# A gated mix of a Fourier layer and a SwiGLU layer: the work up to the second chunk put in a written order

## The chip, the cores and the metric

The kernel runs on one core of a Trainium2 chip. Its time is the device time of one execution in microseconds (us). The time before is the median of three runs.

A core has a matrix engine (TensorE, PE in the profile, with PEld for the loading of its stationary operand), a vector engine (VectorE, DVE), an engine for functions of one operand (ScalarE, ACT), GpSimd (POOL), which only issues stores here, and SyncE (SP), which issues the loads. Each takes its own instructions in the order in which the program has them, and waits at an instruction until what it needs is there. PE writes to eight banks of PSUM; everything else lies in SBUF.

## The reference, cut to what matters

```python
x = A_x                                             # 2048 x 512
g = sigmoid((x * gate_w).sum(-1, keepdims=True))
a = x @ dft_hid_re.T                                # Fourier layer
b = x @ dft_hid_im.T
A = dft_seq_re @ a - dft_seq_im @ b
h = silu(x @ w1) * (x @ w3)                         # SwiGLU layer, F = 1376
B = h @ w2
out = g * A + (1 - g) * B
```

## The kernel before

All is float32. A matrix that is multiplied is split in two parts that PE can take: a *high* part (a copy on ACT, line 108) and a *low* part (the source less the high part, on DVE, line 111). A product of 128x128 by 128x512 is then three matmuls: high by high, high by low, low by high (`mm3`, line 117).

Products of blocks go by a scheme with seven products instead of eight (Strassen's in Winograd's form). Each operand is cut in four blocks, A11 to A22 of the weights and B11 to B22 of x, and sums of blocks are made: T1 = B12 - B11, T2 = B22 - T1, T3 = B22 - B12, T4 = B21 - T2 of x (lines 203 to 207), and four sums of the weights (`sums_wb`, lines 244 to 251). T2, T3 and T4 are written over the raw B11, B12 and B21.

The first stage computes silu(x w1) * (x w3) for the first half of x. It runs over chunks of 128 columns of w1 and w3 (`ITEMS`, line 180). Chunk n has the products X, Y and Z, each a bank of PSUM: X<sub>n</sub> in bank n mod 4, Y<sub>n</sub> in bank 4 + n mod 2, Z<sub>n</sub> in bank 6 + n mod 2. A block of six matmuls (`prod`, line 270) is A11 B11 (`first1`, into X), A12 B21 (`first2`, into Y), and then in `gate_up(n)` (line 332), in this order: X += sum x T2, Z = sum x T3, `first1(n + 3)`, X += sum x T1, Z += a block x T4, `first2(n + 3)`, X += sum x B22. Between them stand ACT's and DVE's work on chunk n and the preparation of the weights of chunk n + 1 (the sums, WB, with `sums_wb`, `high_wb`, `low_wb`) and of chunk n + 4 (the plain blocks, WA). So in `gate_up(1)` chunk 4's `first1` and `first2` are multiplied and the weights of chunk 5 are split; chunk 5's `first1` is multiplied in `gate_up(2)`.

Chunk 0 does without the scheme. `plain` (line 401) computes its four blocks C00, C10, C01, C11 with eight halves of six matmuls each, as the blocks of x arrive: B11, B21, B12, B22. Its result h, 128x1024, is stored by POOL in two halves (`store_h`, line 317). There are two buffers of h: chunk 0 has one, T1 the other, chunk 1 takes chunk 0's.

Weights come as tiles of four blocks of 128x256 (`load_w`, line 221; four such tiles in turn), x as four tiles of 128x1024 (`load_xo`). All loads are on SyncE's queue, in order.

The lines 392 to 488 hold the work up to `gate_up(1)`: loads, eleven matmuls on zeros, chunk 0, A11 B11 and A12 B21 of chunks 1 to 3, the sums and splits of x, and WB of chunk 1. They are written in an order, but the framework's scheduler is free to interleave these lines and does: in the trace, two matmuls of X of chunk 1 stand inside a half of chunk 0. Only from line 674 on (`manual_schedule`) are the instructions of each engine issued as they are written. The lists `early`, `mid` and `at_end` (line 326) hold extra work that `gate_up(n)` runs at three places.

Of the kernel before, what the change touches and what calls it, by code (L numbers as in the profile page):

```python
# [32 lines left out]
def fnet_swiglu_gate_kernel(  # L33
# [46 lines left out]
    def bank(k, name):  # L80
        return psum.tile([P, 512], F32, tag=f"ps{k}", name=name)
# [31 lines left out]
    def split(hi, lo, src):  # L113
        high(hi, src)
        low(hi, lo, src)

    def mm3(ps, ah, al, bh, bl, first, last, chain=False):
        for n, (u, v) in enumerate(((ah, bh), (ah, bl), (al, bh))):
            nc.tensor.matmul(ps, u, v, start=first and n == 0, stop=last and n == 2,  # L119
                             skip_group_check=chain)  # L120
# [115 lines left out]
    def prep_wa(w, lo=0, hi=3):  # L236

        if lo == 0:
            WA[w] = wap.tile([P, 2, 3, 256], F32R, tag="wa", name=f"wa{w}")
        split(*wa_parts(w, lo, hi))  # L240

    WU = {}

    def sums_wb(w):

        r = WS.pop(w)
        u = WU[w] = wup.tile([P, 4, 256], F32, tag="wu", name=f"wu{w}")
        nc.vector.tensor_add(u[:, 0], r[:, 3], r[:, 2])
        nc.vector.tensor_sub(u[:, 1], u[:, 0], r[:, 0])
        nc.vector.tensor_sub(u[:, 2], r[:, 0], r[:, 3])  # L250
        nc.vector.tensor_sub(u[:, 3], r[:, 1], u[:, 1])
# [13 lines left out]
    def prep_wb(w):  # L265
        sums_wb(w)
        high_wb(w)
        low_wb(w)
# [12 lines left out]
    def first1(n):  # L281
        x = bank(n % 4, f"X{n}")
        prod(x, n, 0, 0, True)
        s1 = s1p.tile([P, 512], F32, tag="s1", name=f"s1_{n}")
        nc.scalar.activation(s1, x, AF.Copy)
        G[n] = (x, s1)

    def first2(n):

        y = bank(4 + n % 2, f"Y{n}")  # L290
        prod(y, n, 1, 1, True)
        s1 = G[n][1]
        nc.vector.tensor_add(s1, s1, y)
        put_score(n, 0, s1)
# [28 lines left out]

    early, mid, at_end = {}, {}, {}

    def run(work, n):
        for f in work.get(n, ()):
# [2 lines left out]
    def gate_up(n):  # L332
        last = NI - 1
        x, s1 = G.pop(n)
        z = bank(6 + n % 2, f"Z{n}")
        if n == last - 1:

            u2, g1 = (s1p.tile([P, 512], F32, tag="s1", name=f"{k}_{n}") for k in ("u2", "g1"))
        else:
            h = hp.tile([P, 1024], F32, tag="h", name=f"h{n}")  # L340
            u2, g1 = h[:, :512], h[:, 512:]
        u4 = u4p.tile([P, 512], F32, tag="u4", name=f"u4_{n}")
        nw = WSET[n + 1] if n < last else 0
# [12 lines left out]
        nc.scalar.activation(u2, x, AF.Copy)  # L356
        run(early, n)
        prod(z, n, 5, 5, True, True)
        nc.scalar.activation(u4, z, AF.Copy)
        if nw is not None:  # L360
            sums_wb(nw)
        if n + LOOK <= last:
            first1(n + LOOK)
        if nw is not None:
            high_wb(nw)
        prod(x, n, 3, 3, False, True)
        nc.vector.tensor_add(u4, u4, x)  # L367
        if nw is not None:
            low_wb(nw)
        run(mid, n)  # L370
        prod(z, n, 2, 6, False, True)
        nc.vector.tensor_add(u2, u2, z)
        nc.vector.tensor_mul(u2, s1, u2)  # L373
        store_h(n, 0, u2)
        if wa is not None:
            WA[wa] = wap.tile([P, 2, 3, 256], F32R, tag="wa", name=f"wa{wa}")
# [24 lines left out]
    def plain(b12, a21):  # L401

        c = {}

        def half(i, j, w, x, start):
            if start:
                c[i, j] = bank((0, 4, 6, 7)[2 * i + j], f"C{i}{j}")
            for r in range(2):
                sl = slice(r * P, (r + 1) * P)
                mm3(c[i, j], w(0, sl), w(1, sl), x(r, 0), x(r, 1), start and r == 0,  # L410
                    not start and r == 1)

        def wa(k):
            return lambda h, sl: WA[0][:, h, k, sl]

        def xb(k):
            return lambda q, h: XO[0][:, h, k, q, :]

        w21 = lambda h, sl: a21[:, h, sl]
        x12 = lambda q, h: b12[:, h, q * 512 : (q + 1) * 512]  # L420
        s1 = s1p.tile([P, 512], F32, tag="s1", name="s1_0")
        g1 = u4p.tile([P, 512], F32, tag="u4", name="g1_0")
        h = hp.tile([P, 1024], F32, tag="h", name="h0")
        yield half(0, 0, wa(0), xb(0), True)
        yield half(1, 0, w21, xb(0), True)
        half(0, 0, wa(1), xb(1), False)
        nc.scalar.activation(s1, c[0, 0], AF.Silu)
        yield half(1, 0, wa(2), xb(1), False)
        nc.vector.tensor_mul(h[:, :512], s1, c[1, 0])
        store_h(0, 0, h[:, :512])  # L430
        half(0, 1, wa(0), x12, True)
        yield half(1, 1, w21, x12, True)
        half(0, 1, wa(1), xb(2), False)
        nc.scalar.activation(g1, c[0, 1], AF.Silu)
        half(1, 1, wa(2), xb(2), False)
        nc.vector.tensor_mul(h[:, 512:], g1, c[1, 1])
        yield store_h(0, 1, h[:, 512:])
# [11 lines left out]
    step = plain(b12, a21)  # L449
    prep_wa(0, 0, 1)  # L450
    for q in range(2):
        split(XO[0][:, 0, 0, q], XO[0][:, 1, 0, q], ST[0, "B11"][:, q * 512 : (q + 1) * 512])
    next(step)
    split(a21[:, 0], a21[:, 1], WS[0][:, 3])
    next(step)
    prep_wa(0, 1, 3)
    split_xo(0, "B21")
    next(step)
    split(b12[:, 0], b12[:, 1], ST[0, "B12"])
    next(step)  # L460
    split_xo(0, "B22")
    next(step)
    free(*zt)
    WS.pop(0)
    load_w(4)
    prep_wa(1)
    first1(1)
    first2(1)
    gate1(1)
    sum_xo(0, "T1", hp.tile([P, 1024], F32, tag="h", name="t1"))  # L470
    sum_xo(0, "T2", ST[0, "B11"])
    prep_wa(2)
    first1(2)
    first2(2)
    gate1(2)
    split_xo(0, "T2")
    prep_wb(1)
    sum_xo(0, "T3", ST[0, "B12"])
    split_xo(0, "T3")
    prep_wa(3)  # L480
    first1(3)
    first2(3)
    gate1(3)
    split_xo(0, "T1")
    prep_wa(4)
    sum_xo(0, "T4", ST[0, "B21"])
    split_xo(0, "T4")
    free(*(ST[0, b] for b in ("B11", "B21", "B12", "B22")))

    def do(work, n, f, *a):  # L490
        work.setdefault(n, []).append(lambda: f(*a))


    for k in ("B11", "B21", "B12", "B22"):
# [176 lines left out]
        sum_c(m + LEAD + 1)  # L671
        split_c(m + LEAD)

    ctx.enter_context(tc.manual_schedule())
    for n in range(1, NI):
        gate_up(n)
        if ITEMS[n] == (NC - 1, 0):
# [317 lines left out]
```

## Time and profile before

| | us |
|---|---|
| median of three runs | 711.27 (711.21 to 711.48) |
| profiled execution, its own time | 710.88 |
| span of the profiled execution | 709.1 |
| PE busy | 703.9 (3089 matmuls) |
| DVE busy | 604.6 |
| ACT busy | 369.6 |
| granted PE clock, mean | 1.0 |

The span is that of the instructions on the core; 1.8 us of the execution's time lie around it. Times in the timeline count from the start of the span. A row of it has the start, the duration, the engine, the line, the operation with its output and inputs, and in brackets the idle time of the engine before it with what ended that. `xo` are the split blocks of x, `wa` and `wb` the split weights, `ws` and `xs_B` the raw ones, `C` the banks of chunk 0. Matmuls overlap: one lasts 0.39, and the next starts before it ends. Since line 111 (or 108, or 119) is a helper's, rows of one line are told apart by their tiles.

### The profile page before, as it was taken

To read this page: it belongs to the slowest core of one execution; us is meant where nothing else is said; L and a number is where in the kernel's file an instruction comes from. 1 tells how busy PE (TensorE), PEld (TensorE's weight loads), DVE (VectorE), ACT (ScalarE), POOL (GpSimd) and SP (SyncE) were. 2 spreads that over 40 slices of the span, in tenths; PEclk is the share of its full clock that TensorE was granted. 3 is DMA by queue.
4 is the path that set the end of the run, shared out by engine and by line. 5 is a ranking of instruction groups with operands and counts; after the bars stand their busy time and mean duration, and the time that the engine had idled before them with its cause. 6 is when DMAs were issued, how large, how long until landed. Compare 5 with 4: busy or idle time off the path is not lost.

```text
span 709.1 us, 8589 instructions
## 1 busy us (share of the span) xinstructions
PE 703.9 (99%) x3089; PEld 579.1 (82%) x3089; DVE 604.6 (85%) x733; ACT 369.6 (52%) x478; POOL 64.0 (9%) x118
## 2 busy tenths in 40 slices
PE   9999999999999999999999999999999999999997
PEld 6888888888888888888888888888888888888886
DVE  6979988787679999887999599969997896898985
ACT  6665555655446754454554553544455455455451
POOL 0011111121110000000110001100110000000000
PEclk9999999999999999999999999999999999999999
DMA  7575546589997556712596238814999971773932
GB/s 281 196 295 215 211 188 253 186 313 359 413 412 271 220 207 232 288 60 89 175 358 254 90 122 322 342 48 190 382 419 416 354 270 58 296 285 135 323 119 89
DMA packets 45403, 172.54 MB, mean 243 GB/s; under 512 B 5296, under 2 KB 5424, under 8 KB 41520
## 3 DMA queue, kind: packets, MB, share of 16 engines
q1 hardware_dynamic: 32464, 118.50, 45.2%
q0 software_dynamic: 12608, 52.97, 18.9%
q8 instruction: 24, 0.39, 0.2%
q10 hardware_dynamic: 288, 0.52, 0.2%
q14 instruction: 19, 0.16, 0.1%
HBM read 114.82 MB, written 57.16 MB: 243 GB/s over the span
## 4 chain that ended last, share of the span: by engine, by line
PE 99%; DMA 1%; DVE 0%; ACT 0%; SPq 0%; issue 0%
PE P L119 69%; PE X L119 16%; PE Z L119 8%; PE Y L119 4%; PE C L119 2%; DMA xs_B<-xt 1%; DVE xo L111 0%; DVE zc L788 0%; ACT xo L108 0%; SPq L224 0%
## 5 line engine op out<-in xcount | busy, mean ns | idle before, releaser
L119 PE MATMUL P<-zo,a 128*128 128x512 f32 x1344 | 305.5, 390 | 0.0
L119 PEld LDWEIGHTS P<-zo,a 128*128 128x128 f32 x1344 | 252.1, 188 | 53.2 <-DVE zo L111 1.2
L108 ACT ACTIVATE zo<-B 128x1024 fp32r<-128x1024 f32 (+1 forms) x182 | 189.3, 1045 | 184.5 <-PE P L119 93.2
L111 DVE TENSOR_TENSOR zo<-B,zo 128x1024 fp32r<-128x1024 f32 (+1 forms) x182 | 217.9, 1204 | 48.2 <-ACT zo L108 47.4
L119 PE MATMUL P<-zo,H 128*128 128x512 f32 x468 | 106.2, 389 | 0.0
L119 PEld LDWEIGHTS P<-zo,H 128*128 128x128 f32 x468 | 87.9, 188 | 18.2
L645 DVE TENSOR_TENSOR B<-B,B 128x1024 f32<-128x1024 f32 (+1 forms) x78 | 93.0, 1192 | 0.1
L119 PE MATMUL X<-xo,wb 128*128 128x512 f32 x378 | 92.7, 390 | 0.0
L119 PEld LDWEIGHTS X<-xo,wb 128*128 128x128 f32 x378 | 71.0, 188 | 14.7
L119 PE MATMUL P<-zo,Y 128*128 128x512 f32 x336 | 76.3, 390 | 0.0
L119 PEld LDWEIGHTS P<-zo,Y 128*128 128x128 f32 x336 | 63.1, 188 | 13.1
L322 POOL DMA_DIRECT2D hsp<-h x42 | 23.0, 547 | 126.5 <-DVE h L373 75.6
L119 PE MATMUL X<-xo,wa 128*128 128x512 f32 x126 | 32.3, 390 | 0.0
L119 PE MATMUL Z<-xo,wa 128*128 128x512 f32 x126 | 32.3, 391 | 0.0
L119 PE MATMUL Y<-xo,wa 128*128 128x512 f32 x126 | 32.1, 390 | 0.0
L119 PE MATMUL Z<-xo,wb 128*128 128x512 f32 x126 | 32.1, 390 | 0.0
L648 DVE TENSOR_TENSOR B<-B,B 128x1024 f32<-128x1024 f32 x26 | 31.7, 1219 | 0.0
L863 ACT ACTIVATE zu<-P 128x512 f32<-128x512 f32 x32 | 19.1, 598 | 20.4 <-PE P L119 20.3
L367 DVE TENSOR_TENSOR u<-u,X 128x512 f32<-128x512 f32 x21 | 14.4, 687 | 17.7 <-PE X L119 15.5
L119 PEld LDWEIGHTS Z<-xo,wa 128*128 128x128 f32 x126 | 23.6, 188 | 5.3 <-DVE xo L111 0.4
L119 PEld LDWEIGHTS Y<-xo,wa 128*128 128x128 f32 x126 | 23.7, 188 | 4.9
L119 PEld LDWEIGHTS X<-xo,wa 128*128 128x128 f32 x126 | 23.7, 188 | 4.9
(134 smaller groups left out, 551.3 us busy)
## 6 DMA issues: line engine op xcount, KB each, us to landing
B<-cc SPq DMA_DIRECT2D x64, 512.0 KB, 6.1
hsp<-h POOLq DMA_DIRECT2D x42, 256.0 KB, 3.6
B<-hsp SPq DMA_DIRECT2D x20, 512.0 KB, 9.9
wbsp<-wb POOLq DMA_DIRECT2D x8, 1024.0 KB, 4.3
wb<-wbsp SPq DMA_DIRECT2D x8, 1024.0 KB, 7.8
B<-zsp SPq DMA_DIRECT2D x16, 512.0 KB, 8.4
H<-w2sp SPq DMA_DIRECT2D x6, 1024.0 KB, 9.0
ws<-w SPq DMA_DIRECT2D x11, 512.0 KB, 6.1
```

The lines of the kernel that those rows point to most:

```text
L108: nc.scalar.activation(hi, src, AF.Copy)
L111: nc.vector.tensor_sub(lo, src, hi.bitcast(F32))
L119: nc.tensor.matmul(ps, u, v, start=first and n == 0, stop=last and n == 2, skip_group_check=chain)
L322: nc.gpsimd.dma_start(hsp[g, b + k, j // 2, :, j % 2 * 512 : (j % 2 + 1) * 512], h)
L367: nc.vector.tensor_add(u4, u4, x)
L645: nc.vector.tensor_add(t, t, RAW[blk, b, q][:, :n])
L648: nc.vector.tensor_sub(t, RAW[blk, "B12", q], t)
L863: nc.scalar.activation(U[name][:, r], ps[r], AF.Copy)
```

## The change

1. `manual_schedule` is entered ahead of line 392, so the start too is issued as it is written.
2. The first 128x256 block (A11) of the weights of chunks 1 and 2 is loaded as a piece of its own, ahead of B21.
3. A11 B11 of chunk 1 and of chunk 2 (X1, X2) are multiplied among the halves of chunk 0; Y1 and Y2 after chunk 0, then X3, Y3. The other two blocks of WA of chunks 1 and 2 are split apart from A11.
4. In a half of chunk 0 the second matmul is low weights by high x, the third high weights by low x (before, the other way round).
5. The splits, sums, copies and gates stand in a new order. T4's sum, the low part of T1, the split of T4, the add of Y2, the add of Y3 and the gates of chunks 2 and 3 move into `gate_up(1)`, which has a further list `second`, run behind the copy of Z.

The core of the diff (helpers `first1` and `first2` are cut in two: `prod1`, `copy_x`, `prod2`, `sum_g`):

```diff
+    ctx.enter_context(tc.manual_schedule())
     load_w(0, 0, 1)
     load_xo(0, "B11")
...
+    load_w(1, 0, 1)
     load_w(0, 1, 4)
+    load_w(2, 0, 1)
     load_xo(0, "B21")
     load_xo(0, "B12")
-    load_w(1)
+    load_w(1, 1, 4)
     load_xo(0, "B22")
-    load_w(2)
+    load_w(2, 1, 4)
     load_w(3)
...
+            for n, (u, v) in enumerate(((0, 0), (1, 0), (0, 1))):
+                nc.tensor.matmul(C[i, j], wp(u, sl), xp(r, v), start=start and r == n == 0,
+                                 stop=not start and r == 1 and n == 2)
...
+    new_wa(0)
+    split(*wa_parts(0, 0, 1))
     for q in range(2):
         split(XO[0][:, 0, 0, q], XO[0][:, 1, 0, q], ST[0, "B11"][:, q * 512 : (q + 1) * 512])
+    half(0, 0, 0, 0, True)
+    new_wa(1)
+    split(*wa_parts(1, 0, 1))
+    x1 = prod1(1)
     split(a21[:, 0], a21[:, 1], WS[0][:, 3])
+    half(1, 0, None, 0, True)
+    split(*wa_parts(0, 1, 3))
+    new_wa(2)
+    split(*wa_parts(2, 0, 1))
+    x2 = prod1(2)
     WS.pop(0)
     load_w(4)
+    split_xo(0, "B21")
+    half(0, 0, 1, 1, False)
+    split(b12[:, 0], b12[:, 1], ST[0, "B12"])
+    copy_x(1, x1)
+    half(1, 0, 2, 1, False)
+    split(*wa_parts(1, 1, 3))
+    half(0, 1, 0, None, True)
+    copy_x(2, x2)
+    sums_wb(1)
+    nc.scalar.activation(s1, C[0, 0], AF.Silu)
+    split_xo(0, "B22")
+    half(1, 1, None, None, True)
+    sum_xo(0, "T1", t1)
+    high(*wa_parts(2, 1, 3)[::2])
+    nc.vector.tensor_mul(h0[:, :512], s1, C[1, 0])
+    store_h(0, 0, h0[:, :512])
+    half(0, 1, 1, 2, False)
+    sum_xo(0, "T2", ST[0, "B11"])
+    low(*wa_parts(2, 1, 3))
+    half(1, 1, 2, 2, False)
+    free(*zt)
+    new_wa(3)
+    split(*wa_parts(3, 0, 3))
+    nc.scalar.activation(g1, C[0, 1], AF.Silu)
+    split_xo(0, "T2")
+    y1 = prod2(1)
+    high(*xo_parts(0, "T1")[::2])
+    nc.vector.tensor_mul(h0[:, 512:], g1, C[1, 1])
+    store_h(0, 1, h0[:, 512:])
+    y2 = prod2(2)
+    high_wb(1)
+    sum_g(1, y1)
+    first1(3)
+    sum_xo(0, "T3", ST[0, "B12"])
+    y3 = prod2(3)
+    low_wb(1)
+    split_xo(0, "T3")
     gate1(1)
...
+    new_wa(4)
+    split(*wa_parts(4, 0, 3))
...
+    do(early, 1, sum_xo, 0, "T4", ST[0, "B21"])
+    do(early, 1, lambda: low(*xo_parts(0, "T1")))
+    do(second, 1, lambda: split_xo(0, "T4"))
+    do(second, 1, free, *(ST[0, b] for b in ("B11", "B21", "B12", "B22")))
+    do(second, 1, sum_g, 2, y2)
+    for n, at, y in ((2, 1, None), (3, 1, y3)):
+        if y is not None:
+            do(mid, at, sum_g, n, y)
+        do(mid, at, gate1, n)
...
         prod(z, n, 5, 5, True, True)
         nc.scalar.activation(u4, z, AF.Copy)
+        run(second, n)
         if nw is not None:
             sums_wb(nw)
```

More of the change, by code (lines that the diff above doesn't have):

```diff
@@ L234, in wa_parts, with new_wa @@
         return (*(flat(WA[w][:, h, lo:hi]) for h in range(2)), flat(WS[w][:, lo:hi]))
[L236 to L240, printed above, removed]
+    def new_wa(w):
+        WA[w] = wap.tile([P, 2, 3, 256], F32R, tag="wa", name=f"wa{w}")
     WU = {}
@@ L281, in first1, with prod1, copy_x @@
     def first1(n):
+        copy_x(n, prod1(n))
+    def prod1(n):
         x = bank(n % 4, f"X{n}")
         prod(x, n, 0, 0, True)
+        return x
+    def copy_x(n, x):
         s1 = s1p.tile([P, 512], F32, tag="s1", name=f"s1_{n}")
@@ L288, in first2, with prod2, sum_g @@
     def first2(n):
+        sum_g(n, prod2(n))
+    def prod2(n):
         y = bank(4 + n % 2, f"Y{n}")
         prod(y, n, 1, 1, True)
+        return y
+    def sum_g(n, y):
         s1 = G[n][1]
@@ L322, in store_h @@
         nc.gpsimd.dma_start(hsp[g, b + k, j // 2, :, j % 2 * 512 : (j % 2 + 1) * 512], h)
-    early, mid, at_end = {}, {}, {}
+    early, second, mid, at_end = {}, {}, {}, {}
     def run(work, n):
@@ L375, in gate_up @@
         if wa is not None:
-            WA[wa] = wap.tile([P, 2, 3, 256], F32R, tag="wa", name=f"wa{wa}")
+            new_wa(wa)
             parts_a = wa_parts(wa, 0, 3)
@@ L399, in fnet_swiglu_gate_kernel @@
     nc.scalar.activation(act0, warm[:, :24], AF.Silu)
[L401 to L437, printed above, removed]
+    load_w(1, 0, 1)
     load_w(0, 1, 4)
+    load_w(2, 0, 1)
     load_xo(0, "B21")
     load_xo(0, "B12")
-    load_w(1)
+    load_w(1, 1, 4)
     load_xo(0, "B22")
-    load_w(2)
+    load_w(2, 1, 4)
     load_w(3)
@@ L448, in fnet_swiglu_gate_kernel, with half @@
     b12, a21 = zt[0].rearrange("p h a n -> p h (a n)"), zt[1][:, :, 0]
-    step = plain(b12, a21)
-    prep_wa(0, 0, 1)
+    C = {(i, j): bank((0, 4, 6, 7)[2 * i + j], f"C{i}{j}") for i in range(2) for j in range(2)}
+    def half(i, j, w, x, start):
+        wp = lambda h, sl: a21[:, h, sl] if w is None else WA[0][:, h, w, sl]
+        xp = lambda q, h: b12[:, h, q * 512 : (q + 1) * 512] if x is None else XO[0][:, h, x, q, :]
+        for r in range(2):
+            sl = slice(r * P, (r + 1) * P)
+            for n, (u, v) in enumerate(((0, 0), (1, 0), (0, 1))):
+                nc.tensor.matmul(C[i, j], wp(u, sl), xp(r, v), start=start and r == n == 0,
+                                 stop=not start and r == 1 and n == 2)
@@ L451, in fnet_swiglu_gate_kernel @@
+    s1 = s1p.tile([P, 512], F32, tag="s1", name="s1_0")
+    g1 = u4p.tile([P, 512], F32, tag="u4", name="g1_0")
+    h0 = hp.tile([P, 1024], F32, tag="h", name="h0")
+    t1 = hp.tile([P, 1024], F32, tag="h", name="t1")
+    new_wa(0)
+    split(*wa_parts(0, 0, 1))
     for q in range(2):
         split(XO[0][:, 0, 0, q], XO[0][:, 1, 0, q], ST[0, "B11"][:, q * 512 : (q + 1) * 512])
-    next(step)
+    half(0, 0, 0, 0, True)
+    new_wa(1)
+    split(*wa_parts(1, 0, 1))
+    x1 = prod1(1)
     split(a21[:, 0], a21[:, 1], WS[0][:, 3])
-    next(step)
@@ L456, in fnet_swiglu_gate_kernel @@
[L456 to L463, printed above, removed]
+    half(1, 0, None, 0, True)
[3 more added lines that the diff above has]
+    x2 = prod1(2)
     WS.pop(0)
     load_w(4)
-    prep_wa(1)
-    first1(1)
-    first2(1)
-    gate1(1)
-    sum_xo(0, "T1", hp.tile([P, 1024], F32, tag="h", name="t1"))
-    sum_xo(0, "T2", ST[0, "B11"])
-    prep_wa(2)
@@ L473, in fnet_swiglu_gate_kernel @@
[L473 to L488, printed above, removed]
+    split_xo(0, "B21")
[3 more added lines that the diff above has]
+    half(1, 0, 2, 1, False)
@@ L672, in advance @@
         split_c(m + LEAD)
-    ctx.enter_context(tc.manual_schedule())
     for n in range(1, NI):
```

4 lines of the change are left out of this document (removed).

## The prediction

> **What bounds the kernel now.** I read the page first: busy shares, then the chain that ended last.
>
> ```profile
> PE 703.9 (99%) x3089; PEld 579.1 (82%) x3089; DVE 604.6 (85%) x733; ACT 369.6 (52%) x478; POOL 64.0 (9%) x118
> PE 99%; DMA 1%; DVE 0%; ACT 0%; SPq 0%; issue 0%
> ```
>
> TensorE (PE) is the bound from end to end. The number of products does not change, so the time can fall only where PE stands still, and the change reorders nothing behind chunk 1. So I next took the chain in order of time, from the start to 22 us.
>
> ```profile
> 1.19 3.73 DMA xs_B<-xt
> 4.94 0.64 ACT xo L108
> 5.60 0.70 DVE xo L111
> 6.35 8.95 PE C L119 x37
> ```
>
> Before the first product lies the load of B11, which lands at 1.19 + 3.73 = 4.92. Its place in the queue, second, is unchanged. So the first 5.6 us stay. The timeline of PE then shows what is left to win. Columns: start, duration, operation, count, idle before.
>
> ```profile
> 5.62 0.50 PE L119 MATMUL C<-xo,wa 128*128 128x512 f32 x1
> 6.35 0.50 PE L119 MATMUL C<-xo,wa 128*128 128x512 f32 x1 [0.22 <-DVE xo L111]
> 6.68 0.63 PE L119 MATMUL C<-xo,wa 128*128 128x512 f32 x2
> ...
> 7.62 1.53 PE L119 MATMUL C<-xo,a 128*128 128x512 f32 x6
> ...
> 23.75 0.62 PE L119 MATMUL X<-xo,wb 128*128 128x512 f32 x2
> ...
> 34.03 2.88 PE L119 MATMUL X<-xo,wb 128*128 128x512 f32 x12
> ...
> 43.55 2.88 PE L119 MATMUL X<-xo,wb 128*128 128x512 f32 x12
> ```
>
> Between the last two rows lie 42 products (all of chunk 2 but its last block, plus the last block of chunk 1): 9.52 / 42 = 0.2267 us each, with no stand. I number the products from 0 at 5.62. Row 23.75 is number 76 (48 of chunk 0, 24 for chunks 1 and 2, 4 of chunk 3): without stands it would start at 5.62 + 76 x 0.2267 = 22.85, so 0.90 was lost before it. Row 34.03 is number 120: 44 products on, 33.72 without a stand, so 0.31 more. What PE waited for there:
>
> ```profile
> PEld C L119 <- DVE xo L111: 0.9, 2, 0.5
> PEld Z L119 <- DVE xo L111: 0.4, 1, 0.4
> ```
>
> These are the low parts of B11 and B21 (0.90), and of T4 (0.31). A stand costs its wait and about 0.10 of restart: after 6.35 the next product starts 0.33 later instead of 0.2267. **The whole possible gain here is therefore 0.90 + 0.31 = 1.21 us**, 0.17% of 711. That is under the 0.2% (1.42 us) that I count as no change, about what a measurement of this kernel can tell.
>
> **The change part by part.** *The order in a half of chunk 0.* The low part of the weights is now used second, the low part of x third. Product 1 no longer waits, product 2 waits as before until 6.35. The lost time of the first block is 6.35 - 5.62 - 2 x 0.2267 = 0.28 and 0.10 of restart, 0.38. Block 1 starts at 5.62 + 6 x 0.2267 + 0.38 = 7.36, against 7.62 in the row.
>
> *Loads.* The bytes are the same, two 512 KB loads are cut into 128 and 384 KB, and two small pieces pass ahead of B21. ScalarE's (ACT) rows that a load released give the spacing:
>
> ```profile
> 7.19 1.06 ACT L108 ACTIVATE xo<-xs_B 128x1024 fp32r<-128x1024 f32 x1 [0.27 <-DMA xs_B<-xt]
> 8.46 1.06 ACT L108 ACTIVATE b<-xs_B 128x1024 fp32r<-128x1024 f32 x1 [0.21 <-DMA xs_B<-xt]
> 9.74 0.84 ACT L108 ACTIVATE wa<-ws 128x768 fp32r<-128x768 f32 x1 [0.22 <-DMA ws<-w]
> ...
> 11.03 0.60 ACT L427 ACTIVATE s<-C 128x512 f32<-128x512 f32 x1 [0.44 <-PE C L119]
> 11.53 1.05 ACT L108 ACTIVATE xo<-xs_B 128x1024 fp32r<-128x1024 f32 x1
> 12.47 0.83 ACT L108 ACTIVATE wa<-ws 128x768 fp32r<-128x768 f32 x1
> ```
>
> 512 KB take 1.27, so 128 KB take 0.32 and 384 KB 0.95, if a piece pays no fixed part in a running queue. From 4.92: A11 of chunk 1 at 5.24, the rest of chunk 0's weights 6.19, A11 of chunk 2 6.51, B21 7.78, B12 9.05, B22 11.27. The upper end of a piece is that of a load alone, the very first:
>
> ```profile
> 0.74 0.39 SPq L224 DMA_DIRECT2D ws<-w  x1
> 3.21 0.42 ACT L108 ACTIVATE wa<-ws 128x256 fp32r<-128x256 f32 x1 [0.96 <-DMA ws<-w]
> ```
>
> 3.21 - 0.74 = 2.47. I take 0.32, because three loads in a row came at even distance. B21 is then 0.6 later than now, but its products stand at number 24, due at 7.36 + 18 x 0.2267 = 11.44, since 12 products of chunks 1 and 2 lie ahead of them. Cover: about 1.3 us, so the wait on B21 goes (0.26: the 0.90 less the first block's 7.62 - 5.62 - 6 x 0.2267 = 0.64). SyncE waits for nothing new; the load of chunk 4's weights keeps its place behind the others.
>
> *ScalarE and VectorE in written order.* They do the same work and two more splits each. A start-to-start step I take from a stretch where VectorE (DVE) never stands:
>
> ```profile
> 12.84 1.22 DVE L207 TENSOR_TENSOR t<-xs_B,xs_B 128x1024 f32<-128x1024 f32 x1
> 13.98 1.22 DVE L111 TENSOR_TENSOR xo<-xs_B,xo 128x1024 fp32r<-128x1024 f32 x1
> 15.11 1.22 DVE L207 TENSOR_TENSOR xs_B<-xs_B,t 128x1024 f32<-128x1024 f32 x1
> 16.25 0.95 DVE L111 TENSOR_TENSOR wa<-ws,wa 128x768 fp32r<-128x768 f32 x1
> 17.11 0.42 DVE L249 TENSOR_TENSOR wu<-wu,ws 128x256 f32<-128x256 f32 x1
> 17.46 1.23 DVE L111 TENSOR_TENSOR xo<-xs_B,xo 128x1024 fp32r<-128x1024 f32 x1
> 18.60 0.68 DVE L436 TENSOR_TENSOR h<-g,C 128x512 f32<-128x512 f32 x1
> 19.20 0.42 DVE L250 TENSOR_TENSOR wu<-ws 128x256 f32<-128x256 f32 x1
> ```
>
> 1024 columns 1.14, 768 0.86, 512 0.60, 256 0.35. ACT: 512 from PSUM 0.50, 1024 0.94.
>
> Now the written order. Before B22, DVE has B21's low part at 8.9 (its high follows the landing, 7.8 to 8.9), B12's at 10.1, chunk 1's A at 11.3 and four sums from 11.9, and is free at 13.3. ACT's next instruction is the Silu of C00, which waits for product 29: 7.36 + 23 x 0.2267 + 0.39 (a product's duration, 0.62 - 0.23) = 12.96. Only behind it stands B22's high part, 13.5 to 14.6, though B22 lies there since 11.3. So **DVE stands from 13.3 to 14.6**, and after that it has no reserve. Starts on DVE from there: B22 low 14.6, T1 sum 15.8, product 16.9, T2 sum 17.5, chunk 2's low 18.6, chunk 3's low 19.2, T2 low 20.1, product 21.2, add of Y1 21.8, T3 sum 22.4, WB 1 low 23.6, free 24.7. T3's high waits on ACT behind the copy of X3 (product 77 ends 23.85), so 24.4 to 25.5; T3 low 25.5 to 26.7, chunk 4's low 26.7, T4 sum 27.6, T1 low 28.75 to 30.0, T4 low 30.0 to 31.2, add of Y2 31.1, four sums 31.7, add 33.1, WB 2 low 34.3 (its high waits for the sums), add of Y3 35.4, two of chunk 1 36.0 and 36.7, add of Y4 37.3, chunk 5's low 37.9 to 38.9.
>
> Against these stand PE's due times. T3 low: product 91, 7.36 + 85 x 0.2267 = 26.63; late by 0.14, with restart 0.24. T1 low: product 103, 29.35 + 0.24 = 29.59; late 0.43, with restart 0.53. T4 low: product 109, due 31.5; in time by 0.25, so today's wait of 0.31 goes. Chunk 5's low weights: product 140, 37.74 + 0.77 = 38.51; late 0.4, with restart 0.5 and a little for sums that read one another, 0.55. The same things stand now where they are in time:
>
> ```profile
> 25.34 1.22 DVE L111 TENSOR_TENSOR xo<-t,xo 128x1024 fp32r<-128x1024 f32 x1
> ...
> 30.12 1.23 DVE L111 TENSOR_TENSOR xo<-xs_B,xo 128x1024 fp32r<-128x1024 f32 x1 [0.17 <-ACT xo L108]
> ...
> 36.22 0.95 DVE L111 TENSOR_TENSOR wa<-ws,wa 128x768 fp32r<-128x768 f32 x1
> ```
>
> T1 low (25.3) was 3.4 us earlier, T4 low (30.1) alone was late, chunk 5's low (36.2) 1.7 earlier. Chunk 6 is prepared in time again, so nothing is carried on.
>
> Sum: lost after 0.38 + 0.24 + 0.53 + 0.55 = 1.70; lost before 1.21; **+0.5 us**. The profiled execution took 710.88 (span 709.1, 1.8 around it), so 711.4 in its terms; the median shown is 711.27, 0.39 above, so **711.8**.
>
> The Trainium skill ("TensorE: Matmul & The Clock Gate", Part 1, engine queue depths) states that ACT and DVE are strictly first in, first out, while PE may pull weight loads ahead; this speaks against a written order whose Silu waits ahead of a split that is ready. The trace has the same picture on a smaller scale (ACT stood 0.44 before the Silu at 11.03, B22's high right behind it at 11.53); by the rule the sum is mine, without it DVE's stand of 1.3 would go and the sum would be -0.6 (0.38 and the T3 wait left).
>
> **Rivals.** *A: no waits behind.* If DVE's row is 0.5 us shorter up to T1 low, only 0.38 and perhaps the T3 wait stay: 0.38 - 1.21 = -0.8, 710.5. For it: DVE is busy 85% only, and 0.03 of error per step adds up to 0.45 over the 15 steps. Against: the steps were read off an unbroken run. Chance 0.2.
>
> *B, slower: the small pieces pay a fixed part.* Place: A11 of chunks 1 and 2 ahead of B21. It decides from about 0.9 a piece (B21 at 9.0, where DVE's spare 1.3 is used up). At 1.5 a piece B21 lands at 10.1, DVE's whole row moves by about 0.8, and the time by as much: 712.6; at 2.47, product 6 itself waits until 7.9 and B21 lands at 12.1: the row moves by 2.7, 714.5. Against: the even 1.27. Chance 0.07. The Trainium skill ("DMA: Bandwidth & Descriptors", Anatomy of one DMA) gives about 2.0 us fixed per DMA on the software path, with the advice to batch; taken as added to each piece it would put this case near its upper end. The spacing of 1.27, which is 413 GB/s, speaks against a part paid in series on this queue.
>
> *C, slower: h's buffer.* Chunk 1's first copy (ACT, line 356) writes the buffer of chunk 0's h, whose second store is issued later than now. Rows of the store and, with landing times, of the issues:
>
> ```profile
> 19.59 0.55 POOL L322 DMA_DIRECT2D hsp<-h  x1 [5.66 <-DVE h L436]
> ```
>
> ```profile
> hsp<-h POOLq DMA_DIRECT2D x42, 256.0 KB, 3.6
> zsp<-zs POOLq DMA_DIRECT2D x4, 512.0 KB, 6.6
> ```
>
> Now issued at 19.59, 0.3 behind the end of its product; after the change at about 22.2, landing at 25.8 by the median of 3.6, and the copy is due at 26.7. Behind it on ACT stand the copy of Z, T4's high, X4's copy. From a landing time of 5.7 on, T4's high is later (two copies of 0.50 lie before it, and T4's sum ends at 28.8) and PE waits for T4 low; with 6.6 by 1.0: 712.8. Chance 0.08.
>
> **How the numbers follow.** Forecast (DVE's waits, 711.2 to 712.4) 0.55, A 0.2, B 0.07, C 0.08, and 0.10 for a wait in the new order that I overlooked, half of it dearer than 0.9 us. Faster by over 0.2% needs 1.42 us, more than all stands there: 0.03 for a shift of the first load or of late waits. Slower by over 0.2% (above 712.7): most of B and C, half of the rest, and a tail of the forecast: 0.17. Same: 0.80. The range from 710.4 (A) to 712.9 (C's price) leaves out B's dear end and part of the rest.
>
> **What would show it.** Right: X1's first product near 7.4; DVE idle over 1 us before B22's low part; PE's weight loads waiting for the low part of T1 near 30 and of wa near 38.5; no wait for T4. Wrong: no wait on PE between 8 and 45 us (A), ACT waiting for a load ahead of B21 after 9 us (B), or the line-356 copy released by a DMA (C).

## The result, and the profile after

The changed kernel takes **712.42 us** in the median of 22 runs (711.94 to 713.21); the kernel before, run in turns with it, takes 711.24 in 22 runs. The ratio is 1.0015, with a 95% interval of 1.0009 to 1.0021: 1.18 us slower, on the side forecast, and less than the 0.2% that counts as a difference here. The forecast was 711.8 in a range of 710.4 to 712.9. The profiled execution of the changed kernel took 712.67, with a span of 710.9 and a mean granted clock of 1.0.

The page's line of busy times and the summary of its chain of waits, for the kernel after:

```profile
PE 704.2 (99%) x3089; PEld 578.4 (81%) x3089; DVE 605.0 (85%) x735; ACT 369.2 (52%) x480; POOL 64.2 (9%) x118
PE 96%; DVE 1%; DMA 1%; issue 0%; ACT 0%; SPq 0%; ACTq 0%
```

PE has the same 3089 products and DVE and ACT two splits more each. The chain has 96% of PE where it had 99%: more of it now runs through splits that PE waited for. From 24.60 to 39.70 it leaves PE altogether: the copy of X3 on ACT (24.60), T3's high (25.09), a gate and chunk 4's high (26.66), then DVE's row from 27.43 to chunk 5's low weights (38.82). B22's split is not on it. The start of the chain, in order of time (start, duration, what):

```profile
1.18 4.36 DMA xs_B<-xt
...
5.57 0.64 ACT xo L108
...
6.25 1.92 PE C L433 x6
```

B11, still the second load, landed at 1.18 + 4.36 = 5.54 here, 0.62 later than in the profiled execution before. The six products of the first block have become one row of the chain. What PE's weight loads waited for in the whole execution (total, times, longest), the rows of the zeros before the first product left out:

```profile
PEld C L433 <- ACT xo L108: 1.4, 1, 1.4
PEld P L119 <- DVE zo L111: 1.1, 4, 0.4
PEld X L119 <- DVE xo L111: 0.7, 1, 0.7
PEld X L119 <- DVE wa L111: 0.6, 1, 0.6
PEld Z L119 <- DVE xo L111: 0.4, 1, 0.4
PEld C L433 <- DVE xo L111: 0.4, 1, 0.4
PEld X L119 <- ACT h L390: 0.2, 1, 0.2
PEld X L119 <- DVE u L373: 0.2, 1, 0.2
```

The first row is the start, and the second (1.2 before) lies far behind the change. Of the two waits in chunk 0 one is left (0.4, low B11). Five others lie behind it; T1 low (0.7), chunk 5's low weights (0.6) and T3 low (0.4) are the dear ones. PE's timeline shows each as a late start of the next block (a block of six takes 1.36 without a stand):

```profile
6.25 1.92 PE L433 MATMUL C<-xo,wa 128*128 128x512 f32 x6 [0.94 <-ACT xo L108]
8.01 1.53 PE L119 MATMUL X<-xo,wa 128*128 128x512 f32 x6
...
25.69 1.52 PE L119 MATMUL X<-xo,wb 128*128 128x512 f32 x6
27.05 1.83 PE L119 MATMUL Z<-xo,wb 128*128 128x512 f32 x6
28.72 1.53 PE L119 MATMUL X<-xo,wa 128*128 128x512 f32 x6
30.09 0.39 PE L119 MATMUL X<-xo,wb 128*128 128x512 f32 x1
30.71 1.42 PE L119 MATMUL X<-xo,wb 128*128 128x512 f32 x5 [0.24 <-DVE xo L111]
31.98 1.31 PE L119 MATMUL Z<-xo,wa 128*128 128x512 f32 x5
...
38.86 0.70 PE L119 MATMUL X<-xo,wa 128*128 128x512 f32 x2
39.74 1.21 PE L119 MATMUL X<-xo,wa 128*128 128x512 f32 x4 [0.18 <-DVE wa L111]
40.79 1.55 PE L119 MATMUL X<-xo,wb 128*128 128x512 f32 x6
...
44.90 2.88 PE L119 MATMUL X<-xo,wb 128*128 128x512 f32 x12
```

The block at 27.05 lasts until 28.72, 0.31 too long (T3 low); that at 30.09 until 31.98, 0.53 too long (T1 low); that at 38.86 until 40.79, 0.57 too long (chunk 5's weights). Product 84 (in the kernel after the first with chunk 1's sums; before, eight such products stand ahead of it) starts at 25.69, product 162 (the first of chunk 2's last block in both) at 44.90, which are 19.44 and 38.65 behind the first product. Before, they were 19.94 (25.56, eight products behind the row 23.75) and 37.93 (the row 43.55). **So 0.50 is won ahead of product 84, and 1.22 is lost between the two: 0.72 more.**

That explains 0.72 of 1.18. So I cut each profiled execution in the same places, by the starts of the products in the trace. *First*: start of the first product. *84* and *162*: from the first product to that one. *Rest*: from product 162 to the last product. *Tail*: from the last product's start to the end of the span. The profiled time is their sum (first, 162, rest, tail) and about 1.78. The kernels a, b and c ran in three groups, each on another chip; the last column is the median of the kernel before in the same group.

| kernel | first | 84 | 162 | rest | tail | profiled | median | before, same group |
|---|---|---|---|---|---|---|---|---|
| before | 5.62 | 19.94 | 37.93 | 661.42 | 4.14 | 710.88 | 711.24 | |
| after | 6.25 | 19.45 | 38.65 | 661.47 | 4.53 | 712.67 | 712.42 | 711.24 |
| a1_pieces_behind | 5.73 | 19.43 | 38.63 | 661.45 | 4.52 | 712.11 | 712.13 | 711.29 |
| a2_b22_first | 6.38 | 19.45 | 38.63 | 661.39 | 4.52 | 712.70 | 712.09 | 711.29 |
| a3_t3_first | 5.66 | 19.45 | 38.31 | 661.42 | 4.54 | 711.69 | 712.28 | 711.29 |
| a4_both | 5.78 | 19.43 | 38.27 | 661.36 | 4.53 | 711.71 | 711.72 | 711.29 |
| b1_before_two_more | 6.54 | 19.95 | 37.94 | 661.39 | 4.53 | 712.16 | 711.75 | 711.40 |
| b2_seven_more | 5.66 | 19.45 | 38.61 | 661.39 | 4.07 | 711.50 | 711.50 | 711.40 |
| b3_no_idle | 6.14 | 19.44 | 37.63 | 661.38 | 4.52 | 711.45 | 711.42 | 711.40 |
| b4_no_idle_seven | 5.52 | 19.43 | 37.67 | 661.47 | 4.08 | 710.53 | 710.70 | 711.40 |
| c1_old_half | 6.12 | 19.67 | 38.82 | 661.45 | 4.54 | 712.72 | 712.62 | 711.23 |
| c2_before_half | 5.92 | 19.76 | 39.80 | 661.41 | 4.13 | 713.04 | 713.04 | 711.23 |
| c3_t4_first | 5.64 | 20.01 | 38.09 | 661.38 | 4.08 | 710.97 | 710.42 | 711.23 |

The rest is the same everywhere, within 0.11: nothing is carried on behind product 162, as the prediction had it. Between before and after differ the stands (0.72), the tail (0.39, not foreseen) and, in the profiled executions, the start (0.63). In the medians the first two make 1.11 of 1.18.

### The profile page after: what moved, and what is told of

It reads as the page before. It is cut to its first block, busy times and chain, and to the rows that moved or that the text cites. A ratio compares the mean times of both kernels' runs of the same rounds, so it can differ in the third digit from the quotient of the medians.

```text
span 710.9 us, 8599 instructions
## 1 busy us (share of the span) xinstructions
PE 704.2 (99%) x3089; PEld 578.4 (81%) x3089; DVE 605.0 (85%) x735; ACT 369.2 (52%) x480; POOL 64.2 (9%) x118
## 4 chain that ended last, share of the span: by engine, by line
PE 96%; DVE 1%; DMA 1%; issue 0%; ACT 0%; SPq 0%; ACTq 0%
PE P L119 69%; PE X L119 15%; PE Z L119 7%; PE Y L119 4%; PE C L433 2%; DMA xs_B<-xt 1%; DVE xo L111 0%; DVE s L298 0%; DVE wa L111 0%; DVE xs_B L207 0%; ACT wb L108 0%; ACT xo L108 0%; ACT wa L108 0%; DVE zc L805 0%; ACT s L302 0%
## 5 line engine op out<-in xcount | busy, mean ns | idle before, releaser
L119 PEld LDWEIGHTS Z<-xo,wb 128*128 128x128 f32 x126 | 23.6, 188 | 5.3 <-DVE xo L111 0.4
```

## The experiments

Two things stood open: which part of the written order causes the late splits, and what the start and the tail have to do with the change. The theory for the splits is the prediction's: DVE's stand before B22 low leaves it without reserve. The rival is a second anchor further down the row. For the start, the theory is that the small load right behind B11 holds it back; the rival is that B11's landing varies by itself.

### The small load behind B11: a1_pieces_behind

```diff
-    load_w(1, 0, 1)
     load_w(0, 1, 4)
+    load_w(1, 0, 1)
     load_w(2, 0, 1)
```

> The changed kernel with one line moved: A11 of chunk 1 is loaded behind the rest of chunk 0's weights, not right behind B11. Theory (the small piece right behind B11 holds B11's last packets back): B11 lands near 4.9 as before, the first product starts at 5.6, all else as in the changed kernel, so about 0.6 less than its 712.42: 711.8. Rival (the late landing of 5.54 in the changed kernel's profile is scatter that has nothing to do with the order of the loads): the median stays at 712.4, and B11's landing is early in some kernels and late in others whatever the order.

Measured: 712.13, ratio 1.0012 (1.0004 to 1.0021), first product at 5.73, the rest as after. One landing decides nothing, but others stand beside it: a3 and b2 keep the two loads behind B11 as in the kernel after and have the first product at 5.66, and b1 has the order of before there and has it at 6.54, the latest of all. ACT's row that takes B11, first in b2 (with the two pieces as in the kernel after), then in b1:

```profile
4.98 1.15 ACT L108 ACTIVATE xo<-xs_B 128x512 fp32r<-128x512 f32 x2 [1.44 <-DMA xs_B<-xt]
```

```profile
5.86 1.15 ACT L108 ACTIVATE xo<-xs_B 128x512 fp32r<-128x512 f32 x2 [2.28 <-DMA xs_B<-xt]
```

So the theory falls: the landing scatters over 1.0 us (4.84 to 5.86 on ACT's row over all kernels), whatever lies behind it. The 0.63 of the two profiled executions is no part of the change.

### The Silu ahead of B22, T3 behind X3's copy: a2_b22_first, a3_t3_first, a4_both

```diff
-    nc.scalar.activation(s1, C[0, 0], AF.Silu)
     split_xo(0, "B22")
+    nc.scalar.activation(s1, C[0, 0], AF.Silu)
```

> The changed kernel with the split of B22 put ahead of the Silu of C00 on ScalarE. By the sentence of the prediction (without the Silu ahead of it VectorE's stand before B22's low part goes, and with it the wait on T1): about 0.5 less than 712.42, 711.9. Rival: VectorE's row is anchored anew at T3's low part, which waits for T3's high part, and that stands on ScalarE behind the copy of X3, so the 0.7 won before B22 is only stood off before T3's low part: 712.4, with VectorE idle about 1.5 instead of 0.78 before T3's low part, and the three waits of PE unchanged.

Measured: 712.09, ratio 1.0013 (1.0004 to 1.0022), between the theory's 711.9 and the rival's 712.4; product 162, at 38.63, shows no gain. DVE in a2's timeline:

```profile
14.24 1.22 DVE L111 TENSOR_TENSOR xo<-xs_B,xo 128x1024 fp32r<-128x1024 f32 x1
...
20.82 1.23 DVE L111 TENSOR_TENSOR xo<-xs_B,xo 128x1024 fp32r<-128x1024 f32 x1 [1.01 <-ACT xo L108]
...
26.32 1.23 DVE L111 TENSOR_TENSOR xo<-xs_B,xo 128x1024 fp32r<-128x1024 f32 x1 [0.81 <-ACT xo L108]
```

The stand before B22 low (0.66 in the kernel after) is gone, and a stand of 1.01 has come before T2 low (20.82): T2's high waits on ACT behind the Silu of C01, which waits for PE. The rival had the gain stood off only before T3 low, in a stand of 1.5; that one is 0.81, where it was 0.78 in the kernel after. In that kernel T2's high ended at 19.59 + 1.05 = 20.64, and DVE came to T2 low at 20.71 without a stand, so that the stand before B22 low cost 0.07 at the most. T3 low is one more anchor, since T3's high part waits on ACT behind the copy of X3. The rows of the kernel after, ACT and DVE:

```profile
14.15 1.05 ACT L108 ACTIVATE xo<-xs_B 128x1024 fp32r<-128x1024 f32 x1
15.23 1.23 DVE L111 TENSOR_TENSOR xo<-xs_B,xo 128x1024 fp32r<-128x1024 f32 x1 [0.66 <-ACT xo L108]
...
19.59 1.05 ACT L108 ACTIVATE xo<-xs_B 128x1024 fp32r<-128x1024 f32 x1
20.71 1.22 DVE L111 TENSOR_TENSOR xo<-xs_B,xo 128x1024 fp32r<-128x1024 f32 x1
...
23.05 1.22 DVE L207 TENSOR_TENSOR xs_B<-xs_B,xs_B 128x1024 f32<-128x1024 f32 x1
24.60 0.60 ACT L284 ACTIVATE s<-X 128x512 f32<-128x512 f32 x1 [2.07 <-PE X L119]
25.09 1.05 ACT L108 ACTIVATE xo<-xs_B 128x1024 fp32r<-128x1024 f32 x1
26.18 1.23 DVE L111 TENSOR_TENSOR xo<-xs_B,xo 128x1024 fp32r<-128x1024 f32 x1 [0.78 <-ACT xo L108]
...
29.44 1.22 DVE L111 TENSOR_TENSOR xo<-t,xo 128x1024 fp32r<-128x1024 f32 x1
30.66 1.23 DVE L111 TENSOR_TENSOR xo<-xs_B,xo 128x1024 fp32r<-128x1024 f32 x1
...
38.73 0.95 DVE L111 TENSOR_TENSOR wa<-ws,wa 128x768 fp32r<-128x768 f32 x1
```

T3's sum ends at 23.05 + 1.22 = 24.27, ACT has stood idle for 2.07 up to the copy at 24.60, and T3's high follows at 25.09. The Trainium skill ("TensorE: Matmul & The Clock Gate", Part 1, engine queue depths) has ACT and DVE as strictly first in, first out, and these rows agree: an ACT that had passed the copy could have begun 0.8 earlier. a3 takes that wait away:

```diff
-    first1(3)
+    x3 = prod1(3)
...
-    split_xo(0, "T3")
+    high(*xo_parts(0, "T3")[::2])
+    copy_x(3, x3)
+    low(*xo_parts(0, "T3"))
```

> The changed kernel with T3's high part put ahead of the copy of X3 on ScalarE. Theory (the copy of X3 ahead of T3's high part is what the waits hang on): T3's low part starts about 0.75 earlier, at 25.4; the waits on T3 (0.30) and T1 (0.6) go, the one on chunk 5's low weights stays or grows by 0.1, in all 0.7 to 0.9 less than 712.42: 711.6. Rival (VectorE is simply full from 15 us on): the wait before T3's low part goes but T1's low part moves by less than 0.2, at most 0.3 less: 712.1.

Measured: 712.28, ratio 1.0012 (1.0003 to 1.0021); product 162 at 38.31, a gain of 0.34 in the profile, where the theory had 0.7 to 0.9. PE's wait for T3 low is gone. DVE in a3:

```profile
24.81 1.23 DVE L111 TENSOR_TENSOR xo<-xs_B,xo 128x1024 fp32r<-128x1024 f32 x1
26.55 0.96 DVE L111 TENSOR_TENSOR wa<-ws,wa 128x768 fp32r<-128x768 f32 x1 [0.51 <-ACT wa L108]
```

T3 low no longer stands, and the next instruction does, for 0.51: chunk 4's high (25.68 on ACT in a3) stands behind T3's high, which waits 1.76 for T3's sum, and behind X3's copy and a gate. So of the 0.78 only 0.27 reach T1 low, and the waits on T1 (0.7) and on chunk 5's weights (0.6) stay.

> The changed kernel with both edits, B22's split ahead of the Silu of C00 and T3's high part ahead of the copy of X3. Theory: the two together give more than their sum, since the 0.7 before B22 is no longer stood off: T1's low part and chunk 5's low weights come about 1.4 earlier, all three waits go, 1.4 less than 712.42: 711.0, under the kernel before (711.24). Rival (one of the two carries all): as the better of the two alone, about 711.6.

The edit is a2's and a3's together. Measured: 711.72, ratio 1.0007 (0.9998 to 1.0016); product 162 at 38.27, 0.04 under a3. The two together give no more than a3 alone, as the rival had it; moving the Silu gains nothing behind product 84 in either kernel. The median is 0.56 under a3's though the profiles differ by nothing of that size; I put this down to the scatter of the start, which is argued and not shown.

### Where the late splits end: b3_no_idle, c3_t4_first

b3 is a4 with chunk 4's high part ahead of T3's, and with the add of Y3 in a stand of DVE of 0.5 inside `gate_up(1)`:

```diff
     high_wb(1)
+    new_wa(4)
+    high(*wa_parts(4, 0, 3)[::2])
     sum_g(1, y1)
...
-    new_wa(4)
-    split(*wa_parts(4, 0, 3))
+    low(*wa_parts(4, 0, 3))
...
-            do(mid, at, sum_g, n, y)
+            do(third, at, sum_g, n, y)
```

> The changed kernel with B22's split ahead of the Silu of C00, T3's high part ahead of the copy of X3, and two edits more: chunk 4's high part on ScalarE ahead of T3's (it stood behind a gate that waits), and the add of Y3 on VectorE before chunk 2's WB low part (into the 0.5 in which VectorE stands there). Theory (the waits on T1 and on chunk 5's weights hang on VectorE's stands, each behind an instruction of ScalarE that waits for something else): no stand of PE over 0.1 between 8 and 45 us, 162 products take 37.1 to 37.3 from the first (38.65 in the changed kernel, 37.93 before), 1.4 less than 712.42: 711.0. Rival (VectorE has too much work before T1's low part in any order): at least one wait of 0.4 stays, 162 products take 37.8 or more, 711.6.

Measured: 711.42, ratio 0.9999 (0.999 to 1.0008); product 162 at 37.63, 1.02 earlier than in the kernel after and 0.30 earlier than before. That lies between the theory's 37.1 to 37.3 and the rival's 37.8. The waits behind chunk 0 in b3, and the DVE row that belongs to the first:

```profile
PEld Z L119 <- DVE xo L111: 0.4, 1, 0.4
...
PEld X L119 <- DVE u L373: 0.3, 1, 0.3
```

```profile
30.14 1.23 DVE L111 TENSOR_TENSOR xo<-xs_B,xo 128x1024 fp32r<-128x1024 f32 x1 [0.53 <-ACT xo L108]
```

No wait is left on T3, T1 or chunk 5's weights (0.31, 0.53 and 0.57 in the kernel after). The next in the row is T4 low, whose high stands on ACT behind the copy of Z; its wait of about 0.4 is new, and 1.41 less 0.4 is about the 1.02. **T3's and T1's waits were head-of-line waits on ACT** (a split that is ready, or could be, stands behind an instruction that waits for something else): the one is gone with a3's edit, the other with chunk 4's high ahead of T3's. Chunk 5's wait is gone with the other edit. Counted from the first product, WB 2's low part starts at 28.42 in b3 (34.56 - 6.14) and at 28.48 in a4 (34.26 - 5.78), but chunk 5's low weights behind it start at 31.48 (37.62 - 6.14) and 32.14 (37.92 - 5.78), since the add of Y3 stood between the two in a4 and now fills DVE's stand ahead of them. The two edits of b3 were not run apart; only these rows tell them apart.

c3 is b3 with b2's loads (below), T4's sum ahead of chunk 4's low part and T4's high ahead of the copy of Z:

```diff
+    sum_xo(0, "T4", ST[0, "B21"])
     low(*wa_parts(4, 0, 3))
...
-    do(early, 1, sum_xo, 0, "T4", ST[0, "B21"])
+    do(early, 1, lambda: high(*xo_parts(0, "T4")[::2]))
...
-    do(second, 1, lambda: split_xo(0, "T4"))
+    do(second, 1, lambda: low(*xo_parts(0, "T4")))
```

> The kernel of the run with no idle VectorE and seven loads more (710.7), with T4's sum ahead of chunk 4's low part and T4's high part ahead of the copy of Z on ScalarE. Theory (its last waits, 0.2 to 0.4 on T1's and T4's low parts, hang on T4's high part, which stands on ScalarE behind a copy that waits for PE): 162 products in 37.3 to 37.45 instead of 37.67, 0.3 less: 710.4. Rival (VectorE has no time left there, and T1's low part is as late): 37.6 or more, 710.7.

Measured: **710.42**, ratio 0.9989 (0.998 to 0.9998), as forecast, the fastest of all kernels here, 0.81 under before and by that still inside 0.2%. Product 162 is at 38.09, not at the 37.3 to 37.45 of the theory. PE's waits in c3 and ACT's row that takes B21:

```profile
PEld C L436 <- DVE xo L111: 1.1, 2, 0.6
PEld C L436 <- ACT xo L108: 0.8, 1, 0.8
PEld X L119 <- DVE wa L111: 0.5, 1, 0.5
```

```profile
9.98 1.06 ACT L108 ACTIVATE xo<-xs_B 128x1024 fp32r<-128x1024 f32 x1 [0.85 <-DMA xs_B<-xt]
```

The waits on T4 and on the gate's u are gone, and one on chunk 4's low weights (0.5), which T4's sum now precedes, has come. From product 84 to 162 it takes 18.08, against 18.24 in b4 and 17.99 before. In this execution B21 came late, 4.34 behind the first product (9.98 - 5.64; 2.64 in the kernel after), and PE waited 0.6 for its low part. That is why product 84 is at 20.01. The effect is the one that rival B describes; its cause is told under the loads. The median can't be read off this one profile; why it lies 0.28 under b4's (0.11, when each is taken against the kernel before of its group) isn't shown.

### The tail: b1_before_two_more, b2_seven_more, b4_no_idle_seven

The last DVE row and the span, before and after: 709.1 - 705.40 = 3.70 and 710.9 - 706.79 = 4.11 lie behind the start of the last sum. No work of PE, ACT or DVE lies in that difference.

```profile
705.40 0.69 DVE L788 TENSOR_TENSOR zc<-P,nb 128x512 f32<-128x512 f32 x1 [1.72 <-PE P L119]
```

```profile
706.79 0.69 DVE L805 TENSOR_TENSOR zc<-P,nb 128x512 f32<-128x512 f32 x1 [1.72 <-PE P L119]
```

The trace's records of events have SyncE's last waits there, at eight completion counters of the loads and stores of SP and ACT, in a fixed order and 0.06 apart. The loads and stores use these eight counters in turn. Times from the last product's start:

```
before: last store's counter, seventh of the eight, 3.185; the eighth 3.246; end of the span 4.14
after:  last store's counter, first of the eight,   3.206; the eighth 3.635; end of the span 4.53
```

The theory: the two loads more (two pieces) moved the last store on by two counters, from the seventh to the first, so seven checks instead of one come behind it: six more at 0.06, and with the 0.02 by which that counter itself was passed later 0.39. The rival is a later landing of the last store. By the theory, two more loads in the kernel before must lengthen its tail, and seven more in the kernel after (to the eighth counter) shorten its. b1, on the kernel before:

```diff
-    load_w(3)
+    load_w(3, 0, 1)
+    load_w(3, 1, 4)
...
-    load_w(4)
+    load_w(4, 0, 1)
+    load_w(4, 1, 4)
```

> The kernel before with the weights of chunks 3 and 4 loaded in two pieces each (128 and 384 KB): two loads more, off the path, all else the same. Theory (the 0.4 us that the changed kernel takes longer after its last product comes from the count of loads: the eight completion counters are used in turn, the last store's counter is now the first of the eight that SyncE checks at the end, and the other seven checks of 0.06 follow): 0.39 more than before, and in the trace 4.5 instead of 4.1 between the last product and the end of the span. Rival (the 0.4 belongs to the written order or to the length of the program): no change, and 4.1.

and b2, on the kernel after:

```diff
-    load_w(1, 1, 4)
+    load_w(1, 1, 2)
+    load_w(1, 2, 4)
...
-    load_w(3)
+    for k in range(4):
+        load_w(3, k, k + 1)
...
-    load_w(4)
+    for k in range(4):
+        load_w(4, k, k + 1)
```

> The changed kernel with seven loads more, by cutting the weights of chunks 1 (second part), 3 and 4 into smaller pieces. Theory of the counters: the last store then has the last of the eight counters, no check follows it, 0.45 less than the changed kernel (712.42): about 712.0, and 4.05 between the last product and the end. Rival: as the changed kernel or slower by the extra pieces.

Measured: b1 has a tail of 4.53 (before 4.14) with product 162 where it was (37.94), and 711.75, ratio 1.0005 (0.9996 to 1.0014). b2 has 4.07 (after 4.53) with product 162 at 38.61, and 711.50, ratio 1.0005 (0.9996 to 1.0014). Its median was expected at 712.0; why it came out half a microsecond lower is not shown. The last sum, b1 and b2 (their spans are 710.4 and 709.7):

```profile
706.29 0.69 DVE L790 TENSOR_TENSOR zc<-P,nb 128x512 f32<-128x512 f32 x1 [1.72 <-PE P L119]
```

```profile
706.09 0.69 DVE L808 TENSOR_TENSOR zc<-P,nb 128x512 f32<-128x512 f32 x1 [1.73 <-PE P L119]
```

710.4 - 706.29 = 4.11 and 709.7 - 706.09 = 3.61: the tail follows the number of loads, in both kernels and both directions, by the sizes of the theory. A later landing doesn't do this: the last store's own counter is passed at 3.185 and 3.206.

> Both: the order of the run before this one and the seven loads more. If both theories hold, 0.45 less than that run: 710.6, some 0.7 under the kernel before (711.25). If only one holds, 711.0 to 711.2.

b4 is b3 with b2's loads. Measured: 710.70, ratio 0.9992 (0.9984 to 1.0001), product 162 at 37.67, tail 4.08: 0.72 under b3, of which the tail is 0.44. The gain of the order and that of the tail add up in the trace; where the other 0.28 comes from is not shown.

### The order in a half: c1_old_half, c2_before_half

c1 is the kernel after with the old order of the three products, c2 the kernel before with the new one:

```diff
-            for n, (u, v) in enumerate(((0, 0), (1, 0), (0, 1))):
+            for n, (u, v) in enumerate(((0, 0), (0, 1), (1, 0))):
```

> The changed kernel with the old order in a half of chunk 0 (high weights by low x second). Theory of the prediction (the new order saves one product's step in the first half, 0.23, and nothing else): the first 84 products take 0.23 more than the changed kernel's 19.45, and since T3's low part is anchored to the copy of X3, and T1's low part to T3's, the 162 products too: 38.85 to 38.9, against 38.65. Rival (what is saved early is stood off at T1's low part): 162 products in 38.65, the same.

```diff
-                mm3(c[i, j], w(0, sl), w(1, sl), x(r, 0), x(r, 1), start and r == 0,
-                    not start and r == 1)
+                for n, (u, v) in enumerate(((0, 0), (1, 0), (0, 1))):
+                    nc.tensor.matmul(c[i, j], w(u, sl), x(r, v), start=start and r == n == 0,
+                                     stop=not start and r == 1 and n == 2)
```

> The kernel before with the new order in a half of chunk 0 alone; the scheduler orders some work on VectorE and ScalarE behind it anew. Theory: the first 84 products take 0.23 less than before (19.94), 19.7, and the whole 0.2 less if the new order behind it is no worse: 711.1 against 711.3. Rival: the gain is lost at T4's low part, where PE waits anyway: 162 products in 37.9 as before.

Measured: c1 712.62, ratio 1.0019 (1.001 to 1.0028), product 84 at 19.67, 0.22 later than in the kernel after, 162 at 38.82. c2 713.04 (six runs), ratio 1.0031 (1.002 to 1.0043), product 84 at 19.76, 0.18 earlier than before, but 162 at 39.80, 1.87 later, which neither theory nor rival had. PE's waits in c2 that before doesn't have, or has at 0.4:

```profile
PEld Z L119 <- DVE xo L111: 1.6, 1, 1.6
...
PEld Z L119 <- ACT xo L108: 0.7, 1, 0.7
```

Both belong to T4. T4's sum and low part start at 28.84 and 32.28 on DVE in c2; before, the low part started at 30.12. The order of a half is worth about 0.2 in front, in both kernels. In the kernel before, the scheduler answers the changed lines with another order of the sums and splits behind, which costs ten times as much. So what the written order buys here is also that a change in front leaves the order behind as it is.

## Why the prediction was right, and where it was not

**The possible gain, 1.21, and the front.** Right. Lost up to product 84 are 0.41 (forecast 0.38 in the first block, nothing else), against 0.90 before. X1 starts 1.76 behind the first product (8.01 - 6.25), forecast 1.74.

**The loads.** The step "128 KB take 0.32 ..., if a piece pays no fixed part in a running queue" was off in its premise. ACT's rows that take B21 and B12 in the kernel after:

```profile
8.89 1.06 ACT L108 ACTIVATE xo<-xs_B 128x1024 fp32r<-128x1024 f32 x1 [0.51 <-DMA xs_B<-xt]
...
10.18 1.06 ACT L108 ACTIVATE b<-xs_B 128x1024 fp32r<-128x1024 f32 x1 [0.23 <-DMA xs_B<-xt]
```

B12 follows B21 by 1.29, the old spacing. But ACT took B21 3.32 behind B11 (8.89 - 5.57), against 2.25 before (7.19 - 4.94). Over all kernels it is 2.24 to 2.43 without the two pieces (before, b1, c2) and 2.96 to 5.02 with them, 3.57 in the median of ten. So B21 came about 1.3 later for the two pieces and not 0.64. The DMA engines' rows, before and then after, have the engines' busy share and the GB/s at their ends:

```profile
4.50:5.00 0.50, 0.50 (x2) 0.15 (x1) 0.00 (x0) 0.06 (x1) 0.00 (x0) 1.00 1.02 375
```

```profile
4.50:5.00 0.50, 0.50 (x4) 0.19 (x2) 0.00 (x0) 0.00 (x0) 0.00 (x0) 1.00 0.63 199
```

In each half microsecond from 4.0 to 6.5 the kernel before moves 375 to 434 GB/s and the kernel after 199 to 299. That is 0.34 MB less, 0.8 us at 512 KB in 1.27, and covers the 0.66 that the bytes of the pieces leave open: the queue was not running full while they passed. Where it does run full, further back in b2, seven pieces of 128 KB in a row landed within 2.43 by the records of the landings, 0.35 each, close to the 0.32. Why the engines ran short is not shown; SyncE's rows have the loads issued 0.47 apart, longer than such a piece takes to move. The Trainium skill ("DMA: Bandwidth & Descriptors", Anatomy of one DMA) gives about 2.0 us fixed per DMA on the software path; paid in series by each of the two pieces, that would have been more than any of these runs shows.

The forecast was saved by its cover of 1.3 in front of B21's products. Only c3 has the wait of 0.6, with B21 5.02 behind B11. The first of the 16 DMA engines had finished its share of B21 at 7.99 there, as in all ten kernels with the pieces (7.72 to 8.11; 6.61 to 6.65 in the three without), and the last at 9.96: late engines and not a dearer piece.

**The written order, DVE's timetable.** Its starts, moved by the 0.63 by which the first product was later: B22 low 14.6 + 0.63 = 15.23 (row: 15.23), T3 low 26.13 (26.18), T1 low 29.38 (29.44), T4 low 30.63 (30.66), chunk 5's low 38.53 (38.73). The stand before B22 low was 0.66 and not over 1, because B21, and with it the splits ahead of the stand, came later; its end, which the sum uses, was right to the hundredth. But T2's high, behind the Silu of C01, would have held T2 low at the same place without that stand, which the timetable does not say.

**The late waits.** Right in place and number: T3 low 0.31 (forecast 0.24), T1 low 0.53 (0.53), chunk 5's low weights 0.57 (0.55), none for T4. Two small ones (chunk 1's u and h) add 0.07 and the many small gaps 0.04. With the 0.41 in front that makes 1.93 of stands instead of 1.70, less 1.21: **0.72 instead of the forecast 0.5**. The term was mis-sized by 0.2, no step of it failed.

**"Without it DVE's stand of 1.3 would go and the sum would be -0.6": this failed.** a2 takes the Silu out of the way and gains nothing behind product 84: T2's high stands behind the Silu of C01, which the prediction overlooked, and T3's high behind X3's copy, which its timetable has. The stand that I called the cause cost the row behind it 0.07 at the most. What set the late waits was ACT's row from X3's copy on and DVE's row behind it: b3, which takes three waits away there, gains 1.02. The prediction's picture from the kernel before is also weaker than it reads. By the records of the landings B22 had landed only at 10.99, so that all but 0.04 of ACT's stand of 0.44 before the Silu at 11.03 held nothing back.

**The end of the program** was in no term. The two pieces cost 0.39 there (b1, b2), a third of the 1.18. The prediction counted the pieces at the place where they are loaded and not what every further load does to the order of the closing waits. That, and the 0.2 above, make 0.6 of what separates 711.8 from 712.42.

**Rivals.** A (no waits behind) is refuted by the waits of the kernel after. B (dear pieces): B21 came later than by the bytes, as told under the loads, but without a wait of PE for it in the kernel after. C: ACT's copy at line 361 (356 before) isn't released by a DMA in the kernel after. That only a shift of the first load could make it faster by 0.2% is borne out: the best kernel here, with nearly all of the stands taken away, is 0.11% faster than before.

## What to carry to other kernels

In an order written by hand, look for every instruction that waits for something late and has ready work queued behind it on its engine. A second one may hold the row at the same place, so moving one alone may change nothing (a2), and the timetable has to be worked out again behind each. Where only tenths of a microsecond are at stake, look also at the end of the span: the number of loads and stores in the whole program can move it, at places that no instruction of the change touches. And compare positions from the first product on, not from the span's start, or the scatter of the first load passes for a result.

## What the runs showed of the hardware that I had not expected

- After the last store, SyncE passes eight completion counters one by one, 0.06 each. By which of the eight the last store has, the tail from the last product's start was 4.07 to 4.54 in these kernels, with no work in the difference.
- The landing of the first 512 KB load scattered from 4.84 to 5.86 (ACT's row that takes it) between executions, and with it the whole time; the order of the loads behind it didn't decide it. In the execution of the kernel after that was profiled, two of the 16 DMA engines finished their share of B11 at 5.51 and 5.54 and all others by 4.86. What held these two up stays open.
- Two 128 KB loads near the front of the queue delayed the load behind them by 1.1 to 1.5 us at the first of its DMA engines (0.64 by bytes), while the engines moved 199 to 299 GB/s instead of 375 to 434. Further back in a full queue such a load cost 0.35 (b2).
